# Linear attention beside a dense layer: weighing the queries ahead of the product with kv, in one list of steps

## The chip, the cores and the metric

One core of a Trainium2 chip runs the whole kernel. Its engines are TensorE (PE in the profile, with its weight loads as PEld), VectorE (DVE), ScalarE (ACT), GpSimd (POOL) and SyncE (SP), which here only issues DMAs. The metric is the device time of one execution in microseconds, the median of the runs shown. One execution is also recorded by the hardware profiler; the rows and timelines below come from that one.

## The reference

All inputs are bf16: x is 1 x 2048 x 512; there are 32 heads of 16; the hidden layer has 1792 columns.

```python
def _A_ref(x, wqkv, w_phi, wo):
    B, S, D = x.shape
    H = 32; Dh = D // H
    qkv = (lambda x, *d: x.transpose(*d))((x @ wqkv).reshape(B, S, 3, H, Dh), 2, 0, 3, 1, 4)
    q, k, v = qkv[0], qkv[1], qkv[2]
    pq = jnp.einsum("bhsd,hdf->bhsf", q, w_phi)
    pk = jnp.einsum("bhsd,hdf->bhsf", k, w_phi)
    phi_q = jnp.concatenate([_softmax(pq, axis=-1), _softmax(-pq, axis=-1)], axis=-1)
    phi_k = jnp.concatenate([_softmax(pk, axis=-1), _softmax(-pk, axis=-1)], axis=-1)
    kv = jnp.einsum("bhsf,bhsd->bhfd", phi_k, v)
    z  = jnp.einsum("bhsf->bhf", phi_k)
    num = jnp.einsum("bhqf,bhfd->bhqd", phi_q, kv)
    den = jnp.einsum("bhqf,bhf->bhq", phi_q, z)[..., None] + 1e-6
    o = num / den
    return (lambda x, *d: x.transpose(*d))(o, 0, 2, 1, 3).reshape(B, S, D) @ wo

def _B_ref(x, w1, b1, w2):
    h = jnp.einsum("bsd,df->bsf", x, w1) + b1
    sp = jnp.log1p(jnp.exp(-jnp.abs(h))) + jnp.where(h > 0, h, jnp.zeros_like(h))
    act = h * jnp.tanh(sp)
    return jnp.einsum("bsf,fd->bsd", act, w2)

x = A_x
xn = _layernorm(x, axis=-1)
return x + _A_ref(xn, A_wqkv, A_w_phi, A_wo) + _B_ref(xn, B_w1, B_b1, B_w2)
```

Each head has two softmaxes over its 16 logits, one of p and one of -p. Their concatenation, 32 features, is multiplied with kv and divided by den. Branch B is a dense layer with the Mish function.

## The kernel before

The 2048 tokens are 16 tiles of 128, in 4 groups of 4. All weights and intermediates stay on the core.

**The layers.** The layer norm of a group takes its statistics on VectorE (L133, L135); GpSimd makes one over the root (L136, L139); VectorE or, from group 2 on, GpSimd applies it (`ln_apply`, L145); a DMA transposes two tiles at a time (`ln_turn_dma`, L163). The first group is done at the head of the kernel with TensorE transposes. `fold` (L112) multiplies wqkv with w_phi, so that `project` (L173) gives a tile's logits p at once, 4 products of 128 x 512 into one PSUM bank. `value` projects v and evicts it (L181). `hidden` (L194) is a unit of branch B: 4 products into one bank and a Mish on ScalarE (`activate`, L207); there are 56 units, 14 for each group. `second_layer` (L422) is 14 products a tile into a bank, to which `project_out` (L431) adds the attention's 4; `residual` (L439) adds x on VectorE, and `store` (L447) writes out.

**The slots.** The logits go through eight slots `s` of four tiles: 0 to 3 are keys, 4 to 7 queries. In a slot, the logits are evicted as bf16 (L220). `extremes` builds a maximum tree and a minimum tree over the 16 logits of a head, four halvings each on VectorE (L234, L240), and writes p - max and min - p (L245), for all four tiles at once or, in slots 5 to 7, for two. `exponentials` (L257) is done on ScalarE. For keys `normalise` sums on VectorE (L277), takes reciprocals (L287), doubles them (L288) and multiplies (L292); `accumulate` (L304) adds phi_k times v into kv, one PSUM tile of two banks, 8 products a tile. `mask_kv` (L317, L321) copies the blocks on the diagonal into `kvm`. For queries the exponentials are not divided: `turn` (L266) transposes them by DMA at once.

**The queries' end.** `attend(h, i)` takes tile i of pair h (16 of them). The two unnormalised softmaxes stand in different quarters of the partitions, and each is multiplied with kv by itself, so there are 32 products, each on 32 of the array's 128 rows and with 36 columns (L350). ScalarE evicts the sums (L359) and numerators (L362). `combine` then, on VectorE, makes a factor for each sign from the sums, multiplies the numerators and adds the two (L379 to L403), and a DMA transposes the result (L406) for `project_out`.

**The order.** The scheduler takes the instructions as the program writes them: each engine's queue has the order of the code, and waits are for what an instruction needs. The order is written out by hand: a loop over the slots up to kv, and then calls one by one. PSUM has 8 banks; products take them in turns over several pools (`turns`), and a product waits until the bank's last content was evicted. ScalarE has one table for Mish and one for exp, and loads the other at each change (ACT_TABLE_LOAD). SP issues nearly all DMAs in order, and a DMA whose input isn't ready holds those behind it.

Of the kernel before, what the change touches and what calls it, by code (L numbers as in the profile page):

```python
# [9 lines left out]
BF16 = mybir.dt.bfloat16  # L10
# [4 lines left out]
AX = mybir.AxisListType  # L15


@with_exitstack
def kernel(
# [12 lines left out]
    nc = tc.nc  # L32
# [28 lines left out]
    ps = ctx.enter_context(tc.tile_pool(name="ps", bufs=4, space=PSUM))  # L61
    upper = ExitStack()
    px = upper.enter_context(tc.tile_pool(name="px", bufs=1, space=PSUM))
    turns = [cycle([px, ps, ps, ps, ps])]

    def bank(name, dtype=FP32, pool=None):
        pool = pool or next(turns[0])
        return pool.tile([P, 512], dtype, name=name, tag="mm")

    def three_banks(name, bufs):  # L70
        stack = ExitStack()
        return stack, stack.enter_context(tc.tile_pool(name=name, bufs=bufs, space=PSUM))
# [4 lines left out]
    kvm = persist.tile([P, 8, 36], BF16, name="kvm")  # L77
    wqk = wts.tile([P, KT, 2 * D], BF16, name="wqk")
    wsrc = wts.tile([P, 4, DH], BF16, name="wsrc")
    wv = wts.tile([P, KT, D], BF16, name="wv")  # L80
# [5 lines left out]
    wkp = wts.tile([P, KT, D], BF16, name="wkp")  # L86
# [8 lines left out]
    vext = [vpool.tile([P, TPG, 4, 4, 36], BF16, name=f"vext{i}") for i in range(2)]  # L95
# [11 lines left out]
    def fold(wT, dst, dve, kts=range(KT)):  # L107

        for kt in kts:
            pf = bank("pfold")  # L110
            for j in range(4):
                nc.tensor.matmul(  # L112
                    pf[:, j * P : (j + 1) * P],
                    lhsT=wT[:, j, kt * P : (kt + 1) * P],
                    rhs=Wbd[:, j, :],
                    start=True,
                    stop=True,
                )
            copy = nc.vector.tensor_copy if kt in dve else nc.scalar.copy
            copy(  # L120
                dst[:, kt, :].rearrange("p (b a c) -> p a b c", b=8, a=2),
                pf[:].rearrange("p (a b c) -> p a b c", a=2, b=8),
            )

    def ln_stats(t0, n, between=None):

        stats = lnp.tile([P, TPG, nc.vector.BN_STATS_DIM], FP32, name="stats")
        mv = lnp.tile([P, TPG, nc.vector.BN_AGGR_DIM], FP32, name="mv")
        rstd = lnp.tile([P, TPG], FP32, name="rstd")
        for i in range(n):  # L130
            if i == 1 and between is not None:
                between()
            nc.vector.bn_stats(stats[:, i, :], x_sb[:, t0 + i, :])  # L133
        for i in range(n):
            nc.vector.bn_aggr(mv[:, i, :], stats[:, i, :])  # L135
        nc.gpsimd.tensor_scalar(  # L136
            out=rstd[:, 0:n], in0=mv[:, 0:n, 1], scalar1=1e-5, scalar2=None, op0=ALU.add
        )
        nc.gpsimd.tensor_tensor(out=rstd[:, 0:n], in0=rstd[:, 0:n], in1=mhalf[:, 0:n], op=ALU.pow)  # L139
        return mv, rstd  # L140

    def ln_apply(t0, n, mv, rstd, xn, at):
        engine = nc.gpsimd if t0 > TPG else nc.vector
        for i in range(n):
            engine.tensor_scalar(  # L145
                out=xn[:, at + i, :],
                in0=x_sb[:, t0 + i, :],
                scalar1=mv[:, i, 0:1],
                scalar2=rstd[:, i : i + 1],
                op0=ALU.subtract,  # L150
                op1=ALU.mult,
            )

    def ln_turn_pe(t, xn, i, copy):
# [7 lines left out]
    def ln_turn_dma(t, xn, i):  # L162
        nc.sync.dma_start_transpose(  # L163
            out=xnT[:, t : t + 2, :, :].rearrange("p t k c -> p (t k) c"),
            in_=xn[:, i : i + 2, :].rearrange("p t c -> p (t c)"),
        )
# [12 lines left out]
    def value(t, copy):  # L179
        pv = project(wv, t)  # L180
        copy(  # L181
            vext[(t // TPG) % 2][:, t % TPG, :, :, 0:32].rearrange("p j r c -> p (j r) c"),
            pv.rearrange("p (j c) -> p j c", j=16),
        )

    units = iter([(g, f) for g in range(NG) for f in range(FT)])

    def hidden(n, pool=None, late=None):

        for _ in range(n):  # L190
            g, f = next(units)
            ph = bank("ph", FP32, pool)
            for kt in range(KT):
                nc.tensor.matmul(  # L194
                    ph[:],
                    lhsT=w1_sb[:, kt, f * P : (f + 1) * P],
                    rhs=xnT[:, g * TPG : (g + 1) * TPG, kt, :],
                    start=(kt == 0),
                    stop=(kt == KT - 1),
                )  # L200
            if late is None:
                activate(g, f, ph)
            else:
                late.append((g, f, ph))
# [7 lines left out]
    p_of, e_of, qT_of = {}, {}, {}  # L212

    def logits(s, i, copy):
        if i == 0:
            p_of[s] = smx.tile(
                [P, TPG, 512], BF16, name="p_sb" if s < 7 else "p_last", bufs=1
            )
        pp = project(wkp if s < NG else wqp, (s % NG) * TPG + i)
        copy(p_of[s][:, i, :], pp)  # L220

    def extremes(s, between=None, halves=(slice(0, TPG),)):

        if s not in e_of:
            e_of[s] = epool.tile([P, TPG, 16, 2, 32], BF16, name="e")
        for q in halves:
            n = q.stop - q.start
            e = e_of[s][:, q]
            pv = p_of[s][:, q, :].rearrange("p t (c e) -> p (t c) e", e=16)
            for pl, op in enumerate((ALU.max, ALU.min)):  # L230
                src = pv
                for half in (8, 4, 2):
                    m = smx.tile([P, 128, half], BF16, name=f"m{half}", bufs=1)[:, 0 : n * 32, :]
                    nc.vector.tensor_tensor(  # L234
                        out=m, in0=src[:, :, 0:half], in1=src[:, :, half : 2 * half], op=op
                    )
                    src = m

                m = smx.tile([P, 128, 1, 2], BF16, name="m1", bufs=1)[:, 0 : n * 32]
                nc.vector.tensor_tensor(out=m[:, :, 0, :], in0=src, in1=src[:, :, ::-1], op=op)  # L240
                if pl == 0 and between is not None:
                    between()
                mb = m.rearrange("p (b h) u o -> p b h u o", h=2).to_broadcast([P, n * 16, 2, 8, 2])
                p5 = pv.rearrange("p (b h) (e o) -> p b h e o", h=2, o=2)
                nc.vector.tensor_tensor(  # L245
# [489 lines left out]
```

## Time and profile before

| what | us |
|---|---|
| median of 3 runs | 178.29 (178.07 to 178.30) |
| span of the profiled execution | 176.1 |
| DVE busy | 154.1 |
| ACT busy | 125.4 |
| POOL busy | 28.5 |
| Mish, L207, 56 of 704 ns | 34.6 |
| attends, L350, 512 products | 2.8% of the chain |
| evictions of pnd, L359 and L362, 32 | 20.5 |
| DMA transposes of queries (qT), 16 | issue to landing 3.2 / 4.1 / 5.2 (least, median, most) |
| DMA transposes of outputs (ob), 14 | issue to landing 2.4 |

Busy time counts an engine's instructions from start to end; the time of a group divided by its number is the mean of one. Instructions that follow without a wait start a little before the one ahead ends, so the start-to-start distance in the timeline is the better price of one in a full queue: eight Mishes at 71.09 us take 4.73 us together, 0.59 each, though one is recorded with 0.70. TensorE's products overlap more: one of 512 columns is recorded with 379 ns, and 20 of them stand 4.32 us apart in the chain. The longest waits are these (engine and line, what it waited for, us in total, times, the longest):

```profile
POOL rstd L136 <- DVE mv L135: 27.9, 3, 10.7
ACT ds L359 <- PE pnd L350: 15.8, 11, 2.3
...
DVE x_sb L439 <- PE po L431: 6.2, 12, 1.6
ACT p_last L220 <- PE pproj L173: 5.4, 4, 4.5
ACT e L257 <- DVE e L245: 4.6, 4, 1.9
```

GpSimd waits for work, ScalarE mostly for TensorE's attends behind 100 us, and VectorE for TensorE's last products. TensorE has no wait in this list beyond 1.4 us, at its start.

### The profile page before, as it was taken

To read this page: it belongs to the slowest core of one execution; us is meant where nothing else is said; L and a number is where in the kernel's file an instruction comes from. 1 tells how busy PE (TensorE), PEld (TensorE's weight loads), DVE (VectorE), ACT (ScalarE), POOL (GpSimd) and SP (SyncE) were. 2 spreads that over 40 slices of the span, in tenths; PEclk is the share of its full clock that TensorE was granted. 3 is DMA by queue.
4 is the path that set the end of the run, shared out by engine and by line. 5 is a ranking of instruction groups with operands and counts; after the bars stand their busy time and mean duration, and the time that the engine had idled before them with its cause. 6 is when DMAs were issued, how large, how long until landed. Compare 5 with 4: busy or idle time off the path is not lost.

```text
span 176.1 us, 3589 instructions
## 1 busy us (share of the span) xinstructions
PE 171.1 (97%) x1422; PEld 81.6 (46%) x1422; DVE 154.1 (88%) x308; ACT 125.4 (71%) x176; POOL 28.5 (16%) x40
## 2 busy tenths in 40 slices
PE   6899999999999999999999999999999999999993
PEld 2444444454444545554454444444444444444561
DVE  0989999999999999999999979798789978789953
ACT  3667999999998899989996699489223863544200
POOL 4203039700799400000000000000000000000000
PEclk9999999999999999999999999999999999999999
DMA  5998895330023600000000942919945098394434
GB/s 139 272 416 314 131 348 177 60 61 4 0 49 69 124 0 0 0 0 4 0 0 0 179 92 56 100 29 133 229 119 93 3 170 99 91 121 123 65 89 149
DMA packets 44557, 18.08 MB, mean 103 GB/s; under 512 B 36988, under 2 KB 44028, under 8 KB 44540
## 3 DMA queue, kind: packets, MB, share of 16 engines
q1 hardware_dynamic: 43568, 17.50, 46.6%
q10 hardware_dynamic: 972, 0.35, 0.7%
q8 instruction: 11, 0.18, 0.4%
q14 instruction: 6, 0.05, 0.1%
HBM read 6.84 MB, written 2.10 MB: 51 GB/s over the span
## 4 chain that ended last, share of the span: by engine, by line
PE 93%; DVE 3%; DMA 2%; DVEq 0%; issue 0%
PE po L422 28%; PE ph L194 28%; PE pproj L173 22%; PE po L431 7%; PE pnd L350 3%; PE pkv L304 2%; DMA x_sb<-in_A_x_dram 2%; PE pwide L173 1%; DVE stats L499 1%; DVE x_sb L439 1%; PE pfold L112 1%; DVE xn L512 0%; DVE wkp L120 0%; DVE mv L503 0%; PE ptr L157 0%; DVEq L730 0%
## 5 line engine op out<-in xcount | busy, mean ns | idle before, releaser
L422 PE MATMUL po<-w_sb,acts 128*128 128x512 bf16 (+1 forms) x238 | 51.0, 367 | 0.0
L194 PE MATMUL ph<-xnT,w_sb 128*128 128x512 bf16 x224 | 49.5, 379 | 0.0
L207 ACT ACTIVATE acts<-ph,b1f 128x512 bf16<-128x512 f32 x56 | 34.6, 704 | 2.0 <-PE ph L194 1.9
L257 ACT ACTIVATE e<-e 128x1024 bf16<-128x1024 bf16 (+1 forms) x26 | 31.0, 1250 | 4.6 <-DVE e L245 4.6
L194 PEld LDWEIGHTS <-w_sb 128*128 128x128 bf16 x224 | 21.9, 98 | 26.4 <-issue 0.3
L422 PEld LDWEIGHTS <-acts 128*128 128x128 bf16 x238 | 22.2, 98 | 22.5
L173 PEld LDWEIGHTS <-xnT 128*128 128x128 bf16 x192 | 18.2, 98 | 22.0 <-issue 1.2
L277 DVE TENSOR_REDUCE s<-e 128x128 f32<-128x2048 bf16 (+1 forms) x10 | 18.3, 1850 | 0.0
L359 ACT COPY ds<-pnd 128x128 f32<-128x128 f32 x16 | 4.2, 265 | 17.4 <-PE pnd L350 15.8
L145 POOL TENSOR_SCALAR xn<-x_sb,mv,rstd 128x512 bf16<-128x512 bf16 x8 | 16.6, 2079 | 0.2
L439 DVE TENSOR_TENSOR x_sb<-po,x_sb 128x512 bf16<-128x512 f32 (+1 forms) x17 | 11.0, 658 | 6.2 <-PE po L431 6.2
L431 PE MATMUL po<-wqk,ob 128*128 128x512 bf16 (+1 forms) x68 | 15.0, 367 | 0.0
L173 PE MATMUL pproj<-wv,xnT 128*128 128x512 bf16 x64 | 15.0, 379 | 0.0
L234 DVE TENSOR_TENSOR m<-m 128x256 bf16<-128x256 bf16 (+2 forms) x44 | 13.4, 305 | 1.5
L173 PE MATMUL pproj<-wqk,xnT 128*128 128x512 bf16 x64 | 14.5, 379 | 0.0
L220 ACT CAST p_sb<-pproj 128x512 bf16<-128x512 f32 x20 | 10.7, 585 | 3.4 <-PE pproj L173 1.8
L173 PE MATMUL pproj<-wkp,xnT 128*128 128x512 bf16 x52 | 12.6, 379 | 0.2
L292 DVE TENSOR_TENSOR e<-e,r 128x2048 bf16<-128x2048 bf16 x8 | 10.7, 1337 | 0.3
L234 DVE TENSOR_TENSOR m<-p_sb 128x1024 bf16<-128x1024 bf16 (+1 forms) x18 | 10.2, 566 | 0.0
L431 PEld LDWEIGHTS <-ob 128*128 128x128 bf16 x68 | 6.5, 98 | 6.8 <-DMA ob<-ob 0.3
L245 DVE TENSOR_TENSOR e<-m,p_sb 128x2048 bf16<-128x2048 bf16 (+1 forms) x9 | 8.9, 988 | 0.3
L245 DVE TENSOR_TENSOR e<-p_sb,m 128x2048 bf16<-128x2048 bf16 (+1 forms) x9 | 8.9, 989 | 0.3
(73 smaller groups left out, 175.1 us busy)
## 6 DMA issues: line engine op xcount, KB each, us to landing
w_sb<-in_B_w_dram SPq DMA_DIRECT2D x2, 1792.0 KB, 8.4
out_dram<-x_sb SPq DMA_DIRECT2D x15, 128.0 KB, 1.9
x_sb<-in_A_x_dram SPq DMA_DIRECT2D x1, 1024.0 KB, 11.2
x_sb<-in_A_x_dram SPq DMA_DIRECT2D x1, 512.0 KB, 4.3
wv<-in_A_wqkv_dram SPq DMA_DIRECT2D x1, 512.0 KB, 5.0
wqk<-in_A_wo_dram SPq DMA_DIRECT2D x1, 512.0 KB
x_sb<-in_A_x_dram SPq DMA_DIRECT2D x1, 256.0 KB, 3.2
x_sb<-in_A_x_dram ACTq DMA_DIRECT2D x1, 256.0 KB, 3.5
```

Source lines behind the costliest of these rows:

```text
L145: engine.tensor_scalar(out=xn[:, at + i, :], in0=x_sb[:, t0 + i, :], scalar1=mv[:, i, 0:1], scalar2=rstd[:, i : i + 1], op0=ALU.subtract, ...
L173: nc.tensor.matmul(pp, lhsT=xnT[:, t, kt, :], rhs=w[:, kt, :], start=(kt == 0), stop=(kt == KT - 1),)
L194: nc.tensor.matmul(ph[:], lhsT=w1_sb[:, kt, f * P : (f + 1) * P], rhs=xnT[:, g * TPG : (g + 1) * TPG, kt, :], start=(kt == 0), stop=(kt == ...
L207: nc.scalar.activation(acts[:, f, g * 512 : (g + 1) * 512], ph[:], ACT.Mish, bias=b1f[:, f : f + 1])
L220: copy(p_of[s][:, i, :], pp)
L234: nc.vector.tensor_tensor(out=m, in0=src[:, :, 0:half], in1=src[:, :, half : 2 * half], op=op)
L245: nc.vector.tensor_tensor(out=e[:, :, :, pl, :].rearrange("p t b (h e o) -> p (t b) h e o", h=2, o=2), in0=p5 if pl == 0 else mb, in1=mb i ...
L257: nc.scalar.activation(v, v, ACT.Exp)
L277: nc.vector.reduce_sum(t[:, c : c + n], v[:, 16 * c : 16 * c + 16 * n].rearrange("p (c e) -> p c e", e=16), axis=AX.X,)
L422: nc.tensor.matmul(po[:, c], lhsT=acts[:, f, t * P : (t + 1) * P], rhs=w2_sb[:, f, c], start=(f == 0), stop=False,)
L431: nc.tensor.matmul(po[:, c], lhsT=oT_of[h][:, t % 2 * 4 + j, :], rhs=wo_sb[:, j, c], start=False, stop=(j == 3),)
L439: nc.vector.tensor_tensor(out=y, in0=po[:, c], in1=y, op=ALU.add)
```

## The change

It rewrites the order and three parts of the computation.

- **One list.** The loop over slots and the calls behind it are replaced by `PLAN`, 519 names of steps in one order; `step` calls the function for each. Products and evictions are now separate steps: `unit_1_5` is the product and `unit=_1_5` its Mish; `logits_5_0` the product, `logits=_5_0_0` the eviction; a last digit chooses the engine (0 ScalarE, 1 VectorE for evictions; 0 VectorE, 1 GpSimd, 2 ScalarE for `apply` and `sums`). `second_t_0` and `second_t_1` are the halves of a tile's second layer. PSUM has one pool of six banks in turn, two banks more in the head, and behind it two for kv and later for `pnd`.
- **Queries weighed ahead.** num and den may be scaled by any factor of a token and head. `weigh` multiplies the exponentials of -p by (sum of the exponentials of p) / (sum of those of -p), so that both signs stand in one scale before the transpose. `kvm` gets 68 columns with zeros off the diagonal, and `attend` is 8 products over all 128 rows. `divide` takes reciprocals of the four den columns and multiplies the numerators, both read from PSUM by VectorE; there is no eviction on ScalarE and no `combine`. Each tile's result is transposed by its own DMA (`turn_out`).
- **One tree for p and -p.** In slots 5, 6 and 7 the logits are evicted twice into the tile of the exponentials, as p and as -p (`signed_copy`), and `shifted` builds one maximum tree over both and subtracts it in place. Slot 5's tile is the place of two weights no longer needed.
- **Sums.** Sums of exponentials are now taken tile by tile, 17 of 32 by a reduction on VectorE, 15 by four adds on GpSimd; sums of queries are new.
- **Layer norm.** `apply` is done on VectorE or, with a shift that GpSimd prepares in two more steps, as an Identity activation on ScalarE; none is left on GpSimd.
- Fold copies are without a permutation, and three of the second four go to VectorE. The masks are made early.

The diff, cut to its core:

```diff
+MERGED = (5, 6, 7)
+
+PLAN = """
+spread_6 spread_7 spread_5 value_0 spread_4 value_3 gather_1 value=_0_1 root_1 value_1 value=_3_0
+value=_1_0 unit_0_11 apply_6_2 apply_7_0 plane_0_0 unit_0_9 apply_5_2 turned_6 unit_0_2 unit_0_1
...
+sums_2_3_1 normal_2_0 unit=_2_8 unit_2_5 unit=_2_10 unit_2_2 unit=_2_9 unit=_2_3 unit_1_12 unit=_2_5
...
+value=_15_0 value_14 value_8 fold=_2_1 exp_3_3 value_12 fold=_1_1 sums_2_2_0 exp_3_2 add_2_1
+sums_3_3_1 logits_5_0 value=_8_0 value=_12_1 logits_4_1 value=_14_0 normal_2_1 exp_3_0 unit_3_0
...
+logits_6_0 attend_0_0 second_0_1 divide_0_0 exp_4_3 shift_6_1 out_0_0 attend_0_1 minus=_5_2_0
...
+attend_6_1 project_11 divide_6_1 second_13_1 residual_11 out_6_1 residual_10 attend_7_0 store_9
+second_14_0 divide_7_0 out_7_0 attend_7_1 project_12 divide_7_1 store_11 second_14_1 residual_12
+out_7_1 project_13 store_7 store_5 second_15_1 residual_13 store_12 store_8 store_13 project_14
+store_10 project_15 residual_14 store_14 residual_15 store_15
+"""
...
-    ps = ctx.enter_context(tc.tile_pool(name="ps", bufs=4, space=PSUM))
...
+    ps = ctx.enter_context(tc.tile_pool(name="ps", bufs=6, space=PSUM))
...
+    def root_inverse(g):
+        _, mv, rstd, shift = ln_of[g]
         nc.gpsimd.tensor_scalar(
...
+            out=rstd[:], in0=mv[:, :, 1], scalar1=1e-5, scalar2=None, op0=ALU.add
+        )
+        nc.gpsimd.tensor_tensor(out=rstd[:], in0=rstd[:], in1=mhalf[:], op=ALU.pow)
+        nc.gpsimd.tensor_tensor(out=shift[:], in0=mv[:, :, 0], in1=rstd[:], op=ALU.mult)
+        nc.gpsimd.tensor_scalar(
+            out=shift[:], in0=shift[:], scalar1=-1.0, scalar2=None, op0=ALU.mult
+        )
...
+        if engine is nc.scalar:
+            nc.scalar.activation(
+                xn_of[g][:, i, :], x_sb[:, t, :], ACT.Identity, bias=shift[:, i : i + 1],
+                scale=rstd[:, i : i + 1],
+            )
+            return
...
+    def signed_copy(s, i, pp, sign, engine):
+        to = queries(s)[:, i, :, 0 if sign > 0 else 1, :]
+        pp = pp.rearrange("p (b c) -> p b c", c=32)
+        if engine is nc.scalar:
+            if sign > 0:
+                nc.scalar.copy(to, pp)
+            else:
+                nc.scalar.mul(to, pp, -1.0)
...
+    def shifted(s, q):
+        n = q.stop - q.start
+        v = queries(s)[:, q].rearrange("p t b l (h e) -> p (t b l h) e", h=2)
+        src = v
+        for half in (8, 4, 2):
+            m = smx.tile([P, 128, half], BF16, name=f"m{half}", bufs=1)[:, 0 : n * 64, :]
+            nc.vector.tensor_tensor(
+                out=m, in0=src[:, :, 0:half], in1=src[:, :, half : 2 * half], op=ALU.max
+            )
+            src = m
...
+        nc.vector.tensor_tensor(
+            out=v, in0=v, in1=m.to_broadcast([P, n * 64, 8, 2]), op=ALU.subtract
+        )
...
+        if engine is nc.vector:
+            nc.vector.reduce_sum(out, part, axis=AX.X)
+            return
+        for n in (8, 4, 2, 1):
+            to = smx.tile([P, 64, n], FP32, name=f"t{n}", bufs=1) if n > 1 else out[:, :, None]
+            nc.gpsimd.tensor_tensor(
+                out=to[:], in0=part[:, :, 0:n], in1=part[:, :, n : 2 * n], op=ALU.add
+            )
+            part = to
+
+    def weigh(h):
+
+        s, k = NG + h // 2, h % 2
+        sums = sum_of.pop((s, k))[:].rearrange("p t (b l h) -> p (t b) l h", l=2, h=2)
+        rm = smx.tile([P, 32, 2], FP32, name="rm")
+        r2 = smx.tile([P, 32, 2, 2], BF16, name="rq")
+        nc.vector.reciprocal(rm[:], sums[:, :, 1, :])
+        nc.vector.tensor_tensor(
+            out=r2[:],
+            in0=sums[:, :, 0, :, None].to_broadcast([P, 32, 2, 2]),
+            in1=rm[:, :, :, None].to_broadcast([P, 32, 2, 2]),
+            op=ALU.mult,
+        )
...
+        nc.vector.tensor_tensor(
+            out=minus, in0=minus, in1=r2[:, :, :, None, :].to_broadcast([P, 32, 2, 8, 2]),
+            op=ALU.mult,
+        )
...
     def attend(h, i):
...
+        pnd = later[0].tile([P, 2, 512], FP32, name="pnd", tag="nd")
+        nd_of[h, i] = pnd[:, :, 0:272].rearrange("p u (v c) -> p u v c", c=68)
         for b in range(8):
-            for r in range(4):
-                rows = slice(32 * r, 32 * r + 32)
-                nc.tensor.matmul(
-                    pnd[:, r % 2 * 2 + r // 2, 36 * b : 36 * b + 36],
-                    lhsT=qT_of[h][rows, i, b, :],
-                    rhs=kvm[rows, b, :],
...
+            nc.tensor.matmul(
+                pnd[:, b // 4, 68 * (b % 4) : 68 * (b % 4) + 68],
+                lhsT=qT_of[h][:, i, b, :],
+                rhs=kvm[:, b, :],
+                start=True,
+                stop=True,
+            )
+
+    def divide(h, i):
...
+        r = smx.tile([P, 2, 4, 4], FP32, name="r")
+        nc.vector.reciprocal(r[:], nd[:, :, :, 64:68])
+        nc.vector.tensor_tensor(
+            out=o_t.rearrange("p (u v g d) -> p u v g d", u=2, v=4, g=4),
+            in0=nd[:, :, :, 0:64].rearrange("p u v (g d) -> p u v g d", g=4),
+            in1=r[:, :, :, :, None].to_broadcast([P, 2, 4, 4, 16]),
+            op=ALU.mult,
+        )
+
+    def turn_out(h, i):
+        nc.sync.dma_start_transpose(
+            out=oT_of[h][:, 2 + i, :].rearrange("p (j c) -> p j c", c=P), in_=oT_of[h][:, i, :]
+        )
...
+        elif kind == "kv":
+            mask_kv()
+            kvp.close()
+            later.append(ctx.enter_context(tc.tile_pool(name="pq", bufs=1, space=PSUM)))
...
+    for name in PLAN.split():
+        step(name)
```

In the list `plane_s_0` and `plane_s_1` are the two trees of `extremes`, `shift` is `shifted`, `turned` the transpose of two normalised tiles, `spread`, `gather` and `root` the layer norm's statistics, `add` a tile of `accumulate`, `kv` is `mask_kv`, `wq` loads the weights of the second fold, and `out` is `turn_out`.

More of the change, by code (lines that the diff above doesn't have):

```diff
@@ L60, with bank @@
     PSUM = bass.MemoryType.PSUM
[L61 to L72 removed]
+    ps = ctx.enter_context(tc.tile_pool(name="ps", bufs=6, space=PSUM))
+    turns = [cycle([ps])]
+    def bank(name, dtype=FP32):
+        return next(turns[0]).tile([P, 512], dtype, name=name, tag="mm")
     x_sb = persist.tile([P, NT, D], BF16, name="x_sb")
@@ L125, in ln_stats, with fold @@
[L125 to L134, printed above, removed]
-            nc.vector.bn_aggr(mv[:, i, :], stats[:, i, :])
+    def fold(wT, kt):
+        pf = bank("pfold")
+        for j in range(4):
+            nc.tensor.matmul(
+                pf[:, j * P : (j + 1) * P],
+                lhsT=wT[:, j, kt * P : (kt + 1) * P],
+                rhs=Wbd[:, j, :],
+                start=True,
+                stop=True,
+            )
+        return pf
@@ L209, in activate @@
         )
[L212 to L217, printed above, removed]
-            )
[L219 to L245, printed above, removed]
-                    out=e[:, :, :, pl, :].rearrange("p t b (h e o) -> p (t b) h e o", h=2, o=2),
-                    in0=p5 if pl == 0 else mb,
-                    in1=mb if pl == 0 else p5,
-                    op=ALU.subtract,
-                )
@@ L610 @@
-    first, last = (slice(0, 1),), (slice(1, 2),)
-    low, high = (slice(0, 2),), (slice(2, 4),)
-    exponentials(4)
-    accumulate(3, pk)
-    mask_kv()
-    for i in range(TPG):
-        logits(5, i, act if i == 3 else dve)
-    upper.close()
-    after = ExitStack()
-    turns[0] = cycle([ps])
-    later = [after.enter_context(tc.tile_pool(name="pq", bufs=1, space=PSUM))]
-    second_layer(0)
-    late = []
-    hidden(2, late=late)
-    attend(0, 0)
-    for unit in late:
-        activate(*unit)
```

650 lines of the change are left out of this document (297 added, 353 removed).

## The prediction

> **What bounds the kernel now.** I read the page first, then the chain of waits in order of time, then busy time by stretches, then single stretches of VectorE's and GpSimd's timelines. The page:
>
> ```profile
> PE 171.1 (97%) x1422; PEld 81.6 (46%) x1422; DVE 154.1 (88%) x308; ACT 125.4 (71%) x176; POOL 28.5 (16%) x40
> PE   6899999999999999999999999999999999999993
> ```
>
> TensorE is busy in every slice but the first and the last. The chain says the same in time (start, length, what):
>
> ```profile
> 8.76 1.03 PE pproj L173 x4
> ...
> 16.11 4.32 PE ph L194 x20
> ...
> 38.74 0.99 PE pkv L304 x32
> ...
> 100.20 0.30 PE pnd L350 x32
> ...
> 172.22 1.02 DVE x_sb L439 x2
> ```
>
> From 8.76 to 172.20 it never leaves TensorE: 163.4 us of products without a gap. So only three things can move the end: fewer TensorE microseconds, the 8.8 us ahead, the 3.9 us behind. A wait of TensorE anywhere is added in full. Head (turning, folding, first logits) and tail (residuals of the last two tiles and their stores) are the same steps after the change; I cost them at nothing.
>
> How much room do the others have? Busy time by stretch (columns: length, PE, PEld, DVE, ACT, POOL, granted clock, DMA share, GB/s):
>
> ```profile
> 16.00:40.00 24.00, 24.00 (x139) 11.23 (x138) 23.35 (x37) 23.36 (x30) 9.53 (x6) 1.00 0.59 155
> 40.00:60.00 20.00, 20.00 (x122) 9.62 (x121) 19.28 (x29) 18.38 (x25) 13.95 (x18) 1.00 0.27 53
> 60.00:80.00 20.00, 20.00 (x133) 10.13 (x132) 19.52 (x25) 18.82 (x27) 0.00 (x0) 1.00 0.01 2
> 80.00:100.00 20.00, 20.00 (x121) 9.51 (x119) 19.25 (x33) 17.41 (x24) 0.00 (x0) 1.00 0.16 29
> 100.00:140.00 40.00, 40.00 (x457) 18.13 (x456) 34.10 (x89) 25.90 (x38) 0.00 (x0) 1.00 0.62 99
> ```
>
> Until 100 us VectorE works 81.4 of 84 us and ScalarE 78.0; behind it both have room. The clock is 1.00 throughout. A new list of steps is therefore judged by the first 100 us.
>
> **TensorE's own work.** All groups keep their number (56 hidden units, 44 projections, 128 kv products, 4 folds, second layer, output) except the attends. Now one takes 0.30 us (32 products on quarter arrays), 16 take 4.9. Then it is 8 products of 128x68 on the whole array. The nearest row is L304, whole array, 66 columns: 0.99 us for 32, 31 ns each; times 68/66 and 8 gives 0.26 an attend, 4.1 in all. Gain 0.8. Ends: by columns alone from the 512-wide products (4.32 us for 20, 216 ns) 29 ns, gain 1.2; if the 98 ns of a weight load set the pace, a loss of 7.6, which L304 excludes, since it loads the same 128x128 weights. I take 0.8. Without any wait the span is 176.1 - 0.8 = 175.3.
>
> **VectorE.** Gone: combine, for a tile 0.22 + 0.19 + 0.35 + 0.29 + 0.69 + 0.42 (L379 to L403) = 2.16, times 16 = 34.6. New: divide, 0.35 (L385, 128x32) + 0.69 (L439, 512 from PSUM) = 1.04, times 16 = 16.6; weigh, 0.55 (L385, 128x64) + 0.29 (L387) + 0.69 (L394) = 1.53, times 8 = 12.2. One tree over p and -p costs 0.68 + 0.43 + 0.29 + 0.29 + 1.23 = 2.92 for half a slot against 2 x (0.42 + 0.29 + 0.23 + 0.23 + 0.69) = 3.72, six times: -4.8. Seventeen sums of 1.21 against 18.3: +2.3. Three fold copies, two second evictions, two more applies, one logits copy less: about +3. Net -5 us, nearly all behind 100 us, where it is hidden by TensorE anyway.
>
> **ScalarE** loses the 32 evictions of pnd (4.2 + 16.3 us), all behind 100 us too. It gains 10 of 12 evictions of -p (0.59 each), six applies and four table loads (1.28 each), half of it ahead of 100 us. An apply there has no row: between an L220 copy's 0.51 and a Mish's 0.70, I take 0.60, nearest to both. The Trainium skill, page "ScalarE: Activation LUTs", section "What ACT_TABLE_LOAD costs", says that each pointer operand adds about 93 ns; the Mish row (704 ns, one pointer) agrees, an apply has two, and by that estimate six applies cost 0.6 us more than I take.
>
> **GpSimd** loses eight applies of 2.08 and gains 15 sums, each four adds over 512 + 256 + 128 + 64 results. By L476 (1.15 us for 512) that is 2.2 us, by the four-element L139 (1.08 an instruction) 4.3; I take 2.3, since the large adds dominate. Its price is what it does to VectorE:
>
> ```profile
> 27.71 0.43 DVE L288 COPY r<-r 128x256 bf16<-128x256 bf16 x1
> 28.18 1.67 DVE L292 TENSOR_TENSOR e<-e,r 128x2048 bf16<-128x2048 bf16 x1
> ...
> 33.07 0.29 DVE L288 COPY r<-r 128x256 bf16<-128x256 bf16 x1
> 33.39 1.23 DVE L292 TENSOR_TENSOR e<-e,r 128x2048 bf16<-128x2048 bf16 x1
> ```
>
> In 25.91 to 34.2 and 46.39 to 54.66 GpSimd applies. Of VectorE's four L288 and four L292 in there two each are slowed (0.43 and 0.58 against 0.29, 1.67 twice against 1.23): 1.31 us more on 6.1 us of work, 21%. Then eight sums (18 us) stand ahead of the first attend. At 1.31 us for 16.5 us of GpSimd they cost VectorE 1.4 us; at 21% of the three quarters of its time that are two-input operations, 2.9. I take 2.2.
>
> **The order, at its three tightest places.** I add the rows along each queue. TensorE reaches value_0 at 12.6 (8 of the 24 products behind 10.78); a unit or projection is 0.864. VectorE has apply_7_0 ahead of the first tree, where a tree now covers the wait for rstd: it idles 14.4 to 15.6 (L139's end). ScalarE's first apply needs two more small GpSimd steps (0.23 to 0.34): 16.2.
> - A bank for unit_1_12 is freed by unit=_2_9. ScalarE up to there: 6 x 0.60 + 7 x 1.28 + 31 x 0.588 (10 in 5.88 at 85.91) + 12 x 1.0 + 13 x 0.51 = 49.4, from 16.2: 65.6. TensorE: 58 x 0.864 + 8 x 0.25 = 52.1: 64.7. TensorE waits 0.9.
> - logits_5_0 needs fold=_1_1. VectorE up to there: 8 trees of 2.93, 5 multiplies with reciprocal of 2.47, 6 sums of 1.17, 10 copies of 0.64, 6 applies of 0.37, 8 spreads of 0.61, 2 gathers of 0.4 = 57.2, and 1.0 of waiting for exp_0_0 (ScalarE's rows end it at 29.0, VectorE is there at 28.1): 73.8. TensorE: 61.0, 73.6. It waits 0.2 without GpSimd, 1.6 with five of the eight sums' price.
> - attend_0_0 needs weigh_0 and its transpose. VectorE: 15.6 + 78.6 + 1.8 (waiting for exp_4_0: 92.1 against 90.3) = 96.0, plus 3.2 to 4.1 us to landing (the qT row's least and median): 99.2 to 100.1. TensorE: 12.6 + 87.6 = 100.2. No wait without GpSimd, 1.2 to 2.1 with its 2.2.
>
> These don't add up: once TensorE is late, the next place has that much more time. But a late tree also delays exps and so ScalarE's banks. I take 2.0 us of waits, between the largest single place (1.6 to 2.1) and the sum of the first two (2.5).
>
> Behind 100 us there is room. Divides queue in front of trees on VectorE and out transposes behind qT transposes on SP, but the last product project_15 needs attend_7_1 (TensorE at 165.3) + 1.04 + 2.4 to landing (ob row) = 168.9 and starts at 171.2. pnd keeps one buffer: attend_7_1 waits for divide_7_0, ready at 164.9. So SP's 16 qT, 16 ob and 17 stores cost nothing, unless weigh comes 2 us late.
>
> **Sum:** 176.1 - 0.8 + 2.0 = 177.3 of span. The profiled span is 2.2 below the median 178.29; added back, **179.5**, 0.7% slower.
>
> **The rivals.**
> - *The list holds* (faster). Every lateness above is under 2 us and made of small terms. If applies take 0.51, trees hide from GpSimd (1.3 or less) and exps are early, TensorE waits 0.4 at most: 175.3 to 175.7, **177.5 to 177.9**. For it: that the queues' sums match within 1 us at all three places. Against: no slack anywhere to absorb one late transfer.
> - *Waits eat the gain* (no change). Waits of 0.5 to 1.2: **177.9 to 178.7**.
> - *GpSimd stops the trees.* If each of VectorE's two-input operations stood still while GpSimd reads, eight sums x 2.3 x 0.75 = 13.8 us come onto VectorE ahead of attend_0_0, where it has 0.1 to 1: about 13 on TensorE, **191**. Against: L292 ran from 28.18 to 29.85 inside one apply (27.99 to 30.07) and lost 0.44, not 1.9. The Trainium skill, page "SBUF — State Buffer", section "Who interferes with whom", has this rule (an exclusive lock for the whole instruction); this row speaks against it, though an apply reads one operand and a sum two.
> - *Late chain.* Exp, sums, weigh, transpose, attend in slots 6 and 7: if two sums stand on GpSimd at 4.3 instead of 2.3 (+4) and a transpose lands after 5.2 (the row's most, +1.1), the room of 2 to 3 goes and 2 to 3 more come: **182 to 182.5**.
> - That the change doesn't do what it says is excluded by the queues: 128 attend products in place of 512, no eviction of pnd, 15 sums on GpSimd.
>
> **Chances.** The forecast's case (waits of 1.2 to 3.5, 178.7 to 181.0) 47%, the list holds 22%, no change 15%, GpSimd stops the trees 8%, late chain 8%. About 0.2%, 0.36 us, is what a measurement here can tell: faster 22%, within it 15%, slower 63%. The range goes down to 177.1 (attends' gain of 1.2, no wait) and up to 184.5, past the late chain; the stopped trees stay outside.
>
> **What would show it.** pnd at 0.26 us an attend; TensorE idle before ph or pproj, released by ScalarE's acts or VectorE's fold copies, between 25 and 100 us, about 2 us in all, and none behind it; trees slowed only under GpSimd's adds, by a fifth; a sum of 2.3 us. I am wrong if TensorE has no idle time (then near 177.5), or if the waits lie behind 100 us, or if trees take twice their time.

## The result and the profile after

The changed kernel takes 182.17 us (median of 4 runs, 182.02 to 182.4) against 178.3 for the kernel before (178.07 to 178.36): 1.022 times as long, 95% interval 1.0205 to 1.0234. Its profiled execution has a span of 180.7 us against 176.1.

The first lines are the page's: busy time of each engine, then TensorE in 40 slices.

```profile
PE 170.1 (94%) x1038; PEld 82.3 (46%) x1038; DVE 154.4 (85%) x271; ACT 120.2 (67%) x170; POOL 57.3 (32%) x95
PE   6899998999998879899999999999999999999992
```

TensorE's busy time fell from 171.1 to 170.1 us, but where every slice between the second and the last was a 9 there are now 8s and a 7 between 27 and 77 us (a slice is 4.5 us). By stretches (length, then busy us of PE, PEld, DVE, ACT and POOL, the granted clock, DMA share, GB/s):

```profile
16.00:40.00 24.00, 23.04 (x107) 10.13 (x106) 21.63 (x43) 23.52 (x35) 10.19 (x22) 1.00 0.49 131
40.00:60.00 20.00, 19.20 (x117) 9.13 (x116) 19.16 (x28) 19.91 (x28) 7.59 (x9) 1.00 0.36 80
60.00:80.00 20.00, 17.31 (x126) 8.61 (x124) 19.41 (x26) 15.69 (x23) 6.65 (x9) 1.00 0.00 1
80.00:100.00 20.00, 19.65 (x139) 9.74 (x138) 18.29 (x33) 19.45 (x29) 8.12 (x12) 1.00 0.00 1
100.00:140.00 40.00, 39.62 (x232) 18.54 (x231) 36.99 (x65) 28.05 (x39) 14.22 (x20) 1.00 0.43 83
```

TensorE, which was never idle in these stretches before, lacks 0.96, 0.80, 2.69, 0.35 and 0.38 us: 4.45 of the 5.18 ahead of 80 us. Between 40 and 80 us VectorE is as busy as before (38.6 us against 38.8), and GpSimd, which had nothing to do between 60 and 140 us, now has work in all of them. What TensorE waited for, over the whole span (us in total, times, longest):

```profile
PE pkv L427 <- DVE e L414: 1.9, 2, 1.2
...
PE ph L265 <- ACT acts L275: 1.0, 1, 1.0
PE pproj L250 <- DMA xnT<-xn: 0.8, 1, 0.8
PE ph L265 <- DVE wqk L631: 0.8, 1, 0.8
PE po L509 <- DMA ob<-ob: 0.4, 2, 0.2
```

The largest wait is the key products' (pkv) for exponentials that VectorE has still to multiply by their reciprocal sums (L414). All of TensorE's gaps over 0.03 us from 16 us on add up to 5.18 us. (In runs 5 to 9 below some matmul records are missing from the trace; the holes of 0.05 us that they leave are not counted.) By the chain the last product ends at 176.41 instead of 172.20: 4.2 later is 5.18 of gaps less 0.97 us of products.

Why is L414 late? VectorE's timeline (start, length, engine, line, operation):

```profile
49.50 1.12 DVE L341 TENSOR_TENSOR m<-m 128x256 bf16<-128x256 bf16 x1
...
54.19 0.29 DVE L341 TENSOR_TENSOR m<-m 128x256 bf16<-128x256 bf16 x1
...
59.41 2.20 DVE L414 TENSOR_TENSOR e<-e,r 128x2048 bf16<-128x2048 bf16 x1
...
63.10 1.21 DVE L410 COPY r<-r 128x256 bf16<-128x256 bf16 x1
64.34 1.70 DVE L414 TENSOR_TENSOR e<-e,r 128x2048 bf16<-128x2048 bf16 x1
```

and GpSimd's, in the same execution:

```profile
49.26 1.22 POOL L367 TENSOR_TENSOR t<-e 128x512 f32<-128x512 bf16 x1
50.55 2.07 POOL L367 TENSOR_TENSOR t<-t 128x256 f32<-128x256 f32 x2
...
59.37 1.15 POOL L367 TENSOR_TENSOR t<-e 128x512 f32<-128x512 bf16 x1 [5.85 <-ACT e L353]
...
63.01 1.15 POOL L367 TENSOR_TENSOR t<-e 128x512 f32<-128x512 bf16 x1
```

An L341 of 0.29 us lasts 1.12 where it starts 0.24 us into GpSimd's add of 512 results; it ends at 50.62, just behind the add's end at 50.48. The L414 at 59.41 starts 0.04 us into the next such add, which ends at 60.52; from there to 61.61 is 1.09, close to its undisturbed 1.23. The copy L410 at 63.10 ends 0.15 us behind the third, and the L414 after it (1.70) runs beside the smaller adds. So these instructions stood still until the add was over, rather than ran a fifth slower. The copy L410 has one input, so it is not the two-input operations alone that are held. GpSimd loses as well: the adds of 256 and 128 results take 2.07 us together beside VectorE's two-input work and 1.21 us where they are alone (26.49 in the run with two applies on VectorE). Added over all VectorE rows ahead of 100 us, length less undisturbed length, the loss is 4.8 us, of which 4.1 is there by 73 us and 1.4 is that of copies.

### The profile page after: what moved, and what is told of

Same layout as the page of the kernel before. It is cut to its first block, busy times and chain, and to the rows that moved or that the text cites. A ratio compares the mean times of both kernels' runs of the same rounds, so it can differ in the third digit from the quotient of the medians.

```text
span 180.7 us, 2832 instructions
## 1 busy us (share of the span) xinstructions
PE 170.1 (94%) x1038; PEld 82.3 (46%) x1038; DVE 154.4 (85%) x271; ACT 120.2 (67%) x170; POOL 57.3 (32%) x95
## 4 chain that ended last, share of the span: by engine, by line
PE 42%; DVE 25%; ACT 17%; DMA 4%; issue 2%; POOL 1%; DVEq 0%; ACTq 0%
PE po L500 21%; PE pproj L250 7%; PE po L509 7%; ACT e L353 5%; DVE m L336 5%; DMA ob<-ob 4%; PE ph L265 4%; DVE e L344 4%; DVE e L414 4%; ACT acts L275 3%; ACT L275 3%; ACT L353 2%; DVE r L409 2%; DVE sums L363 2%; PE pnd L464 2%
## 5 line engine op out<-in xcount | busy, mean ns | idle before, releaser
L265 PE MATMUL ph<-xnT,w_sb 128*128 128x512 bf16 x224 | 52.7, 379 | 1.8 <-ACT acts L275 1.0
L367 POOL TENSOR_TENSOR t<-e 128x512 f32<-128x512 bf16 x13 | 16.0, 1228 | 72.5 <-ACT e L353 66.0
L353 ACT ACTIVATE e<-e 128x1024 bf16<-128x1024 bf16 x28 | 28.6, 1053 | 6.8 <-DVE e L323 6.7
L250 PE MATMUL pproj<-wkv,xnT 128*128 128x512 bf16 x128 | 30.5, 379 | 1.0 <-DMA xnT<-xn 0.8
L367 POOL TENSOR_TENSOR t<-t 128x256 f32<-128x256 f32 (+1 forms) x30 | 20.0, 665 | 2.3
L363 DVE TENSOR_REDUCE sums<-e 128x64 f32<-128x1024 bf16 x15 | 17.9, 1209 | 2.8 <-ACT e L353 2.8
L184 DVE BATCH_NORM_STATS2 stats<-x_sb 128x6 f32<-128x512 bf16 x16 | 10.2, 680 | 4.0 <-DMA x_sb<-in_A_x_dram 4.0
L414 DVE TENSOR_TENSOR e<-e,r 128x2048 bf16<-128x2048 bf16 x8 | 11.4, 1425 | 0.3
L480 DVE TENSOR_TENSOR ob<-pnd,r 128x512 bf16<-128x512 f32 x16 | 11.1, 692 | 0.6
L285 ACT CAST p<-pproj 128x512 bf16<-128x512 f32 x17 | 10.1, 594 | 1.5 <-PE pproj L250 1.5
L479 DVE RECIPROCAL r<-pnd 128x32 f32<-128x32 f32 x16 | 5.7, 354 | 6.1 <-PE pnd L464 6.1
```

Source lines behind the costliest of these rows:

```text
L184: nc.vector.bn_stats(ln_of[g][0][:, t % TPG, :], x_sb[:, t, :])
L250: nc.tensor.matmul(pp, lhsT=xnT[:, t, kt, :], rhs=w[:, kt, :], start=(kt == 0), stop=(kt == KT - 1),)
L265: nc.tensor.matmul(ph[:], lhsT=w1_sb[:, kt, f * P : (f + 1) * P], rhs=xnT[:, g * TPG : (g + 1) * TPG, kt, :], start=(kt == 0), stop=(kt == ...
L353: nc.scalar.activation(v, v, ACT.Exp)
L363: nc.vector.reduce_sum(out, part, axis=AX.X)
L367: nc.gpsimd.tensor_tensor(out=to[:], in0=part[:, :, 0:n], in1=part[:, :, n : 2 * n], op=ALU.add)
```

## The experiments

Theory after the result: two things are late, each by itself. GpSimd's adds of two operands hold VectorE's two-input operations, about 4 us of the gaps; and ScalarE is late from its two first applies on, 1 us. Rivals: the sums are late because GpSimd's adds are long, or their price is the small one forecast and the list's order loses the rest. In every run the kernel before was run on the same chip: 178.17 to 178.28 us.

**1. Short sums.** GpSimd makes only the last add of each sum.

```diff
-        for n in (8, 4, 2, 1):
-            to = smx.tile([P, 64, n], FP32, name=f"t{n}", bufs=1) if n > 1 else out[:, :, None]
-            nc.gpsimd.tensor_tensor(
-                out=to[:], in0=part[:, :, 0:n], in1=part[:, :, n : 2 * n], op=ALU.add
-            )
-            part = to
+        nc.gpsimd.tensor_tensor(
+            out=out[:, :, None], in0=part[:, :, 0:1], in1=part[:, :, 1:2], op=ALU.add
+        )
```

> Each GpSimd sum is left with its last add (one add of 64 results in place of four adds of 960; 14 of 16 exponentials are left out of the sum). Port theory: GpSimd's adds of two operands hold VectorE's two-input operations until they end, which cost VectorE 4.8 us ahead of 100 us; without them its trees and multiplies take their unslowed 0.29 and 1.23 us, TensorE's waits fall from 5.2 to 1.0-1.5 us (the one at 31 us for ScalarE's bank stays) and the time is 178.3-178.8. ScalarE theory: banks freed late by slower applies and more table loads drive the waits; the time stays at 181 or above.

Measured: 178.2 us (10 runs, 177.5 to 178.71), ratio 0.9993 (0.9978 to 1.0008). The time is 0.1 us below the range expected. The gaps fall from 5.18 to 1.29 us, the last product ends at 171.93. Of the gaps, 0.80 us is the one at 31 us, behind ScalarE's acts; none waits for L414 any more. VectorE does the same instructions as in the changed kernel in 149.3 us instead of 154.4.

**2. Long, but hardly reading.** GpSimd is busy about as long for a sum as in the changed kernel, mostly with writes: two adds of 64 results and four memsets of 512.

```diff
+        t8 = smx.tile([P, 64, 8], FP32, name="t8", bufs=1)
+        for _ in range(4):
+            nc.gpsimd.memset(t8[:], 0.0)
```

> Each GpSimd sum keeps about its length, but most of it is four memsets that read nothing; only two adds of 64 results read (the sums leave out 13 of 16 exponentials). Port theory: as with the short sums, 178.3-179.0, since only reading of operands holds VectorE. Latency theory: a sum that is ready 3 us after its exp is what makes multiplies and adds late; then 181.5-182.5, as the changed kernel.

Measured: 178.55 us (10 runs), ratio 1.0013 (1.0002 to 1.0024); gaps 1.89 us. GpSimd is busy for 54.7 us (57.3 in the changed kernel), and VectorE for 149.8. Its timeline at the same steps:

```profile
58.01 1.23 DVE L418 TENSOR_TENSOR e<-e,r 128x2048 bf16<-128x2048 bf16 x1
...
60.73 0.34 DVE L414 COPY r<-r 128x256 bf16<-128x256 bf16 x1
61.11 1.22 DVE L418 TENSOR_TENSOR e<-e,r 128x2048 bf16<-128x2048 bf16 x1
```

with GpSimd writing beside the second two:

```profile
59.57 0.31 POOL L366 TENSOR_TENSOR t<-e 128x64 f32<-128x64 bf16 x1 [7.43 <-ACT e L353]
59.81 2.30 POOL L371 MEMSET t<- 128x512 f32 x4
```

(The program is four lines longer: L418 here is L414 of the changed kernel.) The multiply takes 1.22 us under the memsets, so it is not GpSimd's being busy, nor the sums' coming late: that rival falls. What remains of it is 0.35 us of time over the short sums.

**3. Two applies on VectorE.** One digit each in the list: apply_5 and apply_6 go from ScalarE to VectorE.

```diff
-value=_1_0 unit_0_11 apply_6_2 apply_7_0 plane_0_0 unit_0_9 apply_5_2 turned_6 unit_0_2 unit_0_1
+value=_1_0 unit_0_11 apply_6_0 apply_7_0 plane_0_0 unit_0_9 apply_5_0 turned_6 unit_0_2 unit_0_1
```

> apply_5 and apply_6 go from ScalarE to VectorE, nothing else. ScalarE theory: the wait of 0.96 us at 31 us goes and the slide behind it is smaller; 181.0 or less. Port theory: the wait at 31 us goes, but those at 47 to 75 us come from VectorE, which gets 0.8 us more; 181.5-182.3.

Measured: 180.71 us (180.15 to 181.34), ratio 1.0137 (1.0101 to 1.0172), so 1.5 us less than the changed kernel by the medians; its four runs lie in two pairs, at 180.15 and 181.3. The gap at 31 us is gone; 3.63 us are left, of which 0.80 and 1.17 wait for L414 as before. ScalarE's lateness is a cause of its own; by the gaps (5.18 less 3.63) it is somewhat larger than its one gap of 0.96.

**4. The eight early sums back on VectorE** (a digit each, as above; they then cost VectorE 1.2 us apiece).

> The eight GpSimd sums ahead of the first attend become reductions on VectorE. Nothing holds VectorE any more (-4.8 us), but eight reductions of 1.2 us come on (+9.4). Port theory: net +4.6 on VectorE, which has no room there, 185-187. If sums on GpSimd cost more than they take off: below 182.

Measured: 184.61 us (184.36 to 185.44), ratio 1.0361 (1.0328 to 1.0394), 0.4 us below the range expected; gaps 6.70 us. Even at the price found here GpSimd is the cheaper place: eight sums of 1.2 are 9.6 us of VectorE, the hold 4.8.

**5. Short sums and two applies together**, the edits of 1 and 3.

> Both edits at once: a sum on GpSimd is only its last add of 64 results (fifteen sixteenths of each sum are left out), and apply_5 and apply_6 are on VectorE. Theory (two separate causes, GpSimd's two-operand adds holding VectorE, and ScalarE 1 us late from its first applies): TensorE's gaps fall from the 1.29 us of the short sums to 0.3-0.5, the one at 31 us goes, the last product ends near 171.9, time 177.3-177.7. Rival (the applies' gain of 1.5 us was only that a less late list meets GpSimd's adds at better moments): no change from the short sums, 178.2, gaps 1.2-1.3.

Measured: 176.87 us (6 runs, 176.24 to 177.13), ratio 0.992 (0.9907 to 0.9933). Gaps 0.61 us, none over 0.26, the last product at 171.20. It is 0.4 us below the range expected and 1.3 us below the kernel before. The two causes account for 4.6 of the 5.18 us; singly they gave 3.9 and 1.55, more in sum, since each also takes some of the other's.

**6. One operand.** GpSimd's four adds become four instructions of the same sizes and results that read one operand.

```diff
-            nc.gpsimd.tensor_tensor(
-                out=to[:], in0=part[:, :, 0:n], in1=part[:, :, n : 2 * n], op=ALU.add
+            nc.gpsimd.tensor_scalar(
+                out=to[:], in0=part[:, :, 0:n], scalar1=2.0, scalar2=None, op0=ALU.mult
             )
```

> GpSimd's four adds of a sum become four instructions of the same sizes, reading the same tiles through one operand (times 2.0) and writing the same results; left out is that the other half of the exponentials is added. Theory (a GpSimd instruction holds VectorE's two-input operations only when it reads two operands; the one-operand applies of the kernel before cost 0.44 us of an L292's 1.67): VectorE's trees and multiplies under GpSimd keep within 0.5 us of their undisturbed time even if GpSimd's instructions get longer, TensorE's gaps 1.3-2.2 us, 178.2-179.2. Rival (any GpSimd instruction that reads large data holds them until it ends): as the changed kernel, gaps of 4-5 us, 181-182.5, with L341 or L414 ending where a GpSimd instruction ends.

Measured: 179.72 us (179.65 to 179.86), ratio 1.0088 (1.0075 to 1.0101); gaps 2.91 us. That is above the time and the gaps that I expected, by 0.5 us and 0.7 us. But VectorE is far freer than under the adds. Groups of this run (busy us, mean ns):

```profile
L367 POOL TENSOR_SCALAR t<-e 128x512 f32<-128x512 bf16 x13 | 20.5, 1574 | 60.7 <-ACT e L353 60.7
...
L414 DVE TENSOR_TENSOR e<-e,r 128x2048 bf16<-128x2048 bf16 x8 | 10.0, 1245 | 0.3
```

and the same two of the changed kernel:

```profile
L367 POOL TENSOR_TENSOR t<-e 128x512 f32<-128x512 bf16 x13 | 16.0, 1228 | 72.5 <-ACT e L353 66.0 <-DVE stats L184 6.5
...
L414 DVE TENSOR_TENSOR e<-e,r 128x2048 bf16<-128x2048 bf16 x8 | 11.4, 1425 | 0.3
```

GpSimd's instruction is longer (1.57 us against 1.23) and the multiply is shorter (1.245 against 1.425, with 1.23 undisturbed). These multiplies lie beside the smaller instructions of a sum. Under one of 512 results lies a tree step (VectorE's row, then GpSimd's):

```profile
51.23 1.08 DVE L336 TENSOR_TENSOR m<-p 128x1024 bf16<-128x1024 bf16 x1
...
51.12 1.52 POOL L367 TENSOR_SCALAR t<-e 128x512 f32<-128x512 bf16 x1
```

It starts 0.11 us into GpSimd's instruction, takes 1.08 us instead of 0.68, and ends 0.33 us before it: it was slowed, not stopped. By 73 us VectorE has lost 1.0 us, where the adds cost it 4.1.

What is left over the short sums, 1.6 us of gaps, is in part this: at 71 us a hidden unit waits 0.87 us for the bank of a fold copy (0.14 in run 1), and VectorE, not idle for longer than in run 1 up to there, starts that copy at 70.43 instead of 69.47. Behind 100 us, 0.24 us waits for a division and 0.64 for a transpose. The sums come later (GpSimd's four groups have means of 1.574, 0.891, 0.762 and 0.495, 3.7 us a sum), which may be behind these two; that is not shown.

**7. The weighed part in the old order.** The kernel before up to the last key product, all early sums on VectorE and eight applies on GpSimd; from there the changed kernel's steps. No diff is shown, since it joins two whole parts.

> The kernel before up to the last key product, in its own hand-written order (all early sums on VectorE, the late applies on GpSimd, no apply on ScalarE), and from there the changed kernel's part: weighed queries ahead of kv, attends of 8 whole-array products, merged trees, and the list's order for what is left. Theory (the weighing and the whole products are worth their 0.8 us, and the loss lies wholly in the early order): no gap ahead of 90 us, gaps of 0-0.8 behind, last product at 171.4-172.2, time 177.5-178.2, which is faster than both kernels or the same as before. Rival (the chain exp, sums, weigh, transpose, attend is itself too long): gaps of over 1 us between 90 and 165 us ahead of attends or of logits, 179 or more.

Measured: 182.08 us (181.73 to 182.92), ratio 1.022 (1.0207 to 1.0234). No gap ahead of 99 us, as the theory says, but 6.08 us of them between 99 and 135: the rival's case. An attend waits 0.93 and 1.57 us for its qT transpose and 1.33 us for a division, and the second layer 1.08 us for a Mish.

**8. The same with later attends** ("pairs" is the last slot's 32 key products, in run 7 ahead of these steps).

```diff
-exp_4_0 exp_4_1 logits_5_2 logits_5_3 kv logits=_5_2_0 minus=_5_2_0 unit_0 sums_4_0_0
-logits=_5_3_0 unit_1 minus=_5_3_0 sums_4_1_0 weigh_0 turn_0_0 turn_0_1 logits_6_3 logits_6_2
-shift_5_0 unit=_0 unit=_1 logits=_6_3_0 minus=_6_3_0 logits_6_1 logits=_6_2_0 minus=_6_2_0
-logits_6_0 second_0_0 logits=_6_1_0 minus=_6_1_0 logits=_6_0_0 minus=_6_0_0 second_0_1
-attend_0_0 divide_0_0 exp_4_3 shift_6_1 out_0_0 attend_0_1 exp_4_2 second_1_0 logits_7_3
-sums_4_2_1 divide_0_1 exp_6_3 project_0 sums_4_3_0 out_0_1 second_1_1 residual_0 weigh_1 store_0
-second_2_0 shift_6_0 turn_1_0 logits_7_2 exp_5_1 logits_7_1 exp_5_0 turn_1_1 project_1
...
+unit_0 unit_1 unit=_0 unit=_1 pairs logits_5_0 logits=_5_0_0 minus=_5_0_0 logits_5_1 logits=_5_1_0
+minus=_5_1_0 exp_4_0 exp_4_1 logits_5_2 logits_5_3 kv shift_5_0 logits=_5_2_0 minus=_5_2_0
+sums_4_0_0 logits=_5_3_0 minus=_5_3_0 sums_4_1_0 weigh_0 turn_0_0 turn_0_1 logits_6_3 second_0_0
+logits_6_2 logits=_6_3_0 minus=_6_3_0 second_0_1 logits=_6_2_0 minus=_6_2_0 logits_6_1 second_1_0
+exp_4_3 shift_6_1 logits_6_0 exp_4_2 logits=_6_1_0 minus=_6_1_0 attend_0_0 divide_0_0 logits=_6_0_0
+minus=_6_0_0 second_1_1 out_0_0 attend_0_1 logits_7_3 sums_4_2_1 divide_0_1 exp_6_3 project_0
+sums_4_3_0 out_0_1 residual_0 weigh_1 store_0 second_2_0 shift_6_0 turn_1_0 logits_7_2 exp_5_1
...
```

> The old order with the weighed part, with its first steps behind kv put in another order: the two late hidden units and their evictions ahead of the last key products, shift_5_0 ahead of the sums of slot 4, and three halves of the second layer ahead of the first attend. Theory (the 6.3 us of gaps behind 99 us are one late chain, of VectorE idle 4.4 us between 96 and 107 and one eviction behind a table load): gaps 0.5-2.5 us, 177.5-179.6. Rival (VectorE has too much to do behind 96 us, whatever the order): gaps of 4 us and more, only further back, 180-182.

Measured: 185.05 us (184.91 to 185.97), ratio 1.0394 (1.0367 to 1.0422); gaps 6.92 us, one of 4.03 at 116. The theory fails. Two rows of TensorE, ahead of that gap and behind it:

```profile
112.02 1.67 PE L482 MATMUL po<-w_sb,acts 128*128 128x512 bf16 x7
...
120.32 3.15 PE L482 MATMUL po<-w_sb,acts 128*128 128x512 bf16 x7 [4.03 <-ACT e L302]
```

Seven products take 3.15 us where seven took 1.67: the granted clock falls to 0.50 within the wait, is 0.50 from 119.5 to 126 us and 1.00 again from 127. All four runs have a mean clock of 0.981 to 0.991, so the slow stretch is a part of what this order costs. The long gap belongs to this order as well: the products wait for a bank that ScalarE empties, and ScalarE is idle for 8.53 us ahead of that, by the profile for VectorE's sums. So the run does not show that every order fails, and the rival stands only as far as these two orders can show it.

In the old order VectorE ends the trees that the first weighing needs at 95 us; in run 5, where GpSimd has the sums (cut short), at 89. I take it that what the old order gains ahead of kv it lacks behind it, since the weighing ahead of kv needs the room that the sums on GpSimd make; this is argued, not shown.

**9. Five applies on GpSimd**, on top of run 3, in its idle time from 34 us on.

```diff
-apply_10_2 unit=_0_12 turned_10 plane_1_0 unit_0_4 unit=_0_3 unit_1_13 unit=_1_0 value=_6_0
-logits_2_0 unit=_1_13 unit_1_3 apply_15_2 apply_12_0 unit=_0_4 plane_1_1 logits_2_1 logits=_2_0_0
-apply_14_2 logits_2_3 logits=_2_1_0 turned_14 value_11 unit=_1_3 add_0_0 normal_0_1 wo logits_2_2
+apply_10_1 unit=_0_12 turned_10 plane_1_0 unit_0_4 unit=_0_3 unit_1_13 unit=_1_0 value=_6_0
+logits_2_0 unit=_1_13 unit_1_3 apply_15_1 unit=_0_4 plane_1_1 logits_2_1 logits=_2_0_0
+apply_14_1 apply_13_1 apply_12_1 logits_2_3 logits=_2_1_0 turned_14 turned_12 value_11 unit=_1_3 add_0_0 normal_0_1 wo logits_2_2
-unit_1_10 unit=_1_7 apply_13_0 unit_1_8 plane_2_1 turned_12 unit=_0_10 unit=_0_13 unit_2_0
+unit_1_10 unit=_1_7 unit_1_8 plane_2_1 unit=_0_10 unit=_0_13 unit_2_0
```

> The run with two applies on VectorE, and beside it apply_10, 15, 14, 13 and 12 moved to GpSimd's idle time between 34 and 44 us (a one-operand instruction of 2.08 us each in the kernel before), with turned_12 right behind. It takes 0.9 us off VectorE and 2.1 us off ScalarE and brings turned_12 some 6 us earlier. Theory (GpSimd work that reads one operand is nearly free for VectorE): gaps from 3.62 to 2.2-2.9 us, the one at 54 us gone, time 179.3-180.0. Rival (any GpSimd work costs VectorE as much as it saves): gaps of 3.4 us or more, 180.5-181.5.

Measured: 180.97 us (180.71 to 181.1), ratio 1.0157 (1.014 to 1.0174), no better than run 3's 180.71; gaps 3.00 us, now one of 2.59 for L414 at 59 us. Fewer gaps gave no less time, since the granted clock falls here too: it is 0.50 from 61.5 to 64.5 us, behind the long wait, and four products that begin at 62.07 take 1.69 us to the next instead of 0.86. All four runs have a mean clock of 0.987 to 0.990. By the last product less the gaps (171.98 against 170.80 in run 3) that costs about 1 us, an estimate, so without it the time would be near 180.0, the upper end of the theory's range. The applies took

```profile
34.03 13.27 POOL L224 TENSOR_SCALAR xn<-x_sb,mv,rstd 128x512 bf16<-128x512 bf16 x5
47.28 1.49 POOL L367 TENSOR_TENSOR t<-e 128x512 f32<-128x512 bf16 x1
```

2.65 us each, not 2.08. VectorE's own loss under them is small: a copy of 0.68 instead of 0.29 and two pairs of tree steps of 1.12 instead of 0.75, 1.1 us in 13.3 us. But the first sum of the next slot starts at 47.28 instead of 44.60, and then meets a tree: the two steps that take 0.75 take 2.00 us at 47.78. So the gain in work was lost again, to one-operand work, to where it pushed the adds, and to the clock behind the one long wait.

## Why the prediction was off

The direction was right, and so was the place of the loss: TensorE waits, ahead of 100 us, for VectorE and ScalarE, and nothing of weight behind; 0.38 us of gaps lie behind 100 us. The size was not: 3.9 us slower by the medians against 1.2 forecast, 5.18 us of waits against 2.0. That 182.17 lies in the late chain's 182 to 182.5 is luck: that chain was to be late in slots 6 and 7, behind 100 us, and it wasn't.

- **The attends** were right: from start to start one takes 0.257 us against 0.305, 0.77 for 16 where I took 0.8. TensorE's last product less its gaps is 171.23 against 172.20, 0.97 earlier, but that this is close to 0.8 is luck. Two terms that I did not have nearly cancel. In the kernel before, the products behind an attend lost another 0.1 us (ten at 100.51 take 2.27 us, at 0.216 each they would take 2.16), 1.4 us in all. And the hidden, projection and key products take 1.3 us more now, in part behind the waits (20 behind the one at 31 us take 4.48 instead of 4.32).
- **GpSimd's price on VectorE, taken at 2.2 us, is the step that failed.** The runs show 4.8 us ahead of 100 us in the rows, and 3.9 us of TensorE's gaps that go with the adds (run 1). I scaled it from eight applies, which read one operand, to adds, which read two. The rows of before showed a fifth; run 6 shows that the kind of instruction decides, not the time for which GpSimd is busy: one-operand instructions that are longer leave the multiply at 1.245 us and cost VectorE 1.2 us ahead of 100 us.
- The rival "GpSimd stops the trees" had the mechanism: operations do stand still until an add ends. Its price was wrong in the other direction, 13.8 us for 4.8. It let VectorE lose three quarters of the adds' time; it loses 4.8 of some 24 us (eight sums of 2.99). Not all of the adds meet a two-input operation: much of that time VectorE spends on its own sums, reciprocals and evictions, which showed no loss, and where GpSimd comes second it is GpSimd that gets slower. The Trainium skill, page "SBUF — State Buffer", section "Who interferes with whom", has the rule that I set aside: a VectorE instruction with two SBUF inputs contends with a GpSimd instruction that reads SBUF, and the second to come is blocked for the other's whole length. For the adds of 512 results this trace agrees (2.20 us for 1.23, until the add's end). For GpSimd's one-operand instructions the runs do not (0.40 us lost under one of 1.52 in run 6, 0.44 us under one of 2.08 before), and the measurement decides.
- **A sum of 2.3 us** was too short: undisturbed it takes 2.65 (1.15 + 1.21 + 0.29), as run, 2.99 on average (1.228 + 0.788 + 0.542 + 0.434). The small adds weigh more than I gave them.
- **An apply on ScalarE at 0.60** was too short as well: 0.72 from one to the next (the first two in 1.52 us, each 0.80 to 0.81 busy). The estimate from the Trainium skill's page "ScalarE: Activation LUTs", section "What ACT_TABLE_LOAD costs", 0.1 us more for the second pointer, agrees. By itself that is 0.2 us at 31 us; but the gap there is 0.96, and moving two applies gave 1.5. I had looked for ScalarE's lateness at unit_1_12, after 31 evictions, and not behind its change back to the Mish table at 29.96 us, which is where it struck.
- **The three tight places** gave no hit: logits_5_0, unit_1_12 and attend_0_0 waited for nothing. VectorE's fold copies were late as I had it, but they struck earlier in the list: the 0.77 us at 74 us is unit_1_11, which waits for the bank of fold=_0_1; logits_5_0 comes at 79 us. The key products, which wait for L414, and turned_12's transpose, behind apply_13 on VectorE, were not on my list, though 2.7 us of the gaps are theirs. I checked where the queue sums were closest, not where the adds would fall.
- Execution by execution the time is 1.7 us above the span here and 2.0 to 2.2 in the kernel before, which makes the result look 0.4 us better than the spans do.

Without these two terms the list holds: run 5, at 176.87, is below the lower end of that case (177.5), but it leaves out most of the sums. No complete version of the sums reached it, and none of the runs beats the kernel before with all its work in. GpSimd's lock may belong to the two operands or to that kind of instruction as such; the runs don't tell these two apart.

## What to carry to other kernels

Work that goes to GpSimd has two prices: its own time, and what it stops on VectorE. Take the second from rows of the same kind of GpSimd instruction, and count the VectorE operations that fall under it (here those with two inputs in SBUF, and a copy), each held until the other ends; a rate from one-operand work says nothing about adds. Where one engine's room is made by another engine's help, as the weighing ahead of kv by the sums on GpSimd, the parts of a change can't be judged one by one. And one long wait of TensorE can cost more than its length, as runs 8 and 9 show: add up the products behind it, not the gaps alone.

## What was not expected of the hardware

GpSimd's memsets of 512 results (about 0.57 us each, four in 2.30) and its one-operand instructions left VectorE's two-input multiply at 1.22 to 1.245 us, while an add of 1.15 us held it for 0.97. TensorE's granted clock fell to 0.50 in the two waits of over 2 us, 2.59 (run 9) and 4.03 us (run 8), and stayed there for 3.4 and 6.8 us, into the products behind them; in the waits of 1.57 (run 7), 1.68 (run 4) and 1.83 us (run 8, at 107 us) it stayed at 1.00. A GpSimd apply took 2.08 us in the kernel before and 2.65 beside VectorE's trees in run 9: there GpSimd was the one that lost.
